# Batch 0 in pieces: keys as floats over SP, W_in in six loads, halves of tokens in the second softmax and first layer, and a new written order

## The chip, the cores and the metric

The kernel runs on one NeuronCore of a Trainium2 chip. Its engines are TensorE (PE; weight loads are shown as PEld), VectorE (DVE), ScalarE (ACT), GpSimd (POOL) and SyncE (SP). Each works through its own list of instructions, whose waits on semaphores hold up what stands behind them in the list. The core has 16 DMA engines, fed here from the queues of POOL, SP and, for the last store, ACT. The metric is the device time of one execution in microseconds, 251.08 us before the change (median of three runs, 250.28 to 251.39).

## The reference

Eight batches, eight heads, 576 tokens, head size 64, and 32 packed queries `p` per head. First `p` attends to `k` and `v`, then `q` attends to the packed result; the outcome, 4608 tokens by 512, goes through two layers with a squared ReLU between them.

```
def sm_attn(qq, kk, vv):
    s = scale * np.matmul(qq, kk.transpose(0, 1, 3, 2))
    s = s - np.max(s, axis=-1, keepdims=True)
    a = np.exp(s)
    a = a / (np.sum(a, axis=-1, keepdims=True) + 1e-09)
    return np.matmul(a, vv)
p_packed = sm_attn(p, k, v)
out = sm_attn(q, p_packed, p_packed)
...
h = x @ w_in            # x: 4608 x 512, w_in: 512 x 2048
r = np.maximum(h, 0.0)
g = r * r
return (g @ w_out).astype(np.float32)
```

## The kernel before

Work goes by batch and by quad, four heads of a batch (two quads). The second attention's product with the packed values is folded into the weights: `wp` is the packed values times W_in (32 x 4 rows for a quad, 2048 columns), and the first layer multiplies the second softmax `a2T` with `wp`. The second layer works on tiles of 128 tokens, `tt` 0 to 35, and 16 blocks `fb` of 128 hidden columns; `gT` holds the squared activations of four batches.

Nothing is scheduled by a planner at build time: the string `ORDER` is a list of words, read from left to right, and each word issues one step's instructions on its engines. So each engine's order is the order of the words that touch it. Digits after a word are batch and quad; a suffix `:a`, `:v`, `:p` names the engine (ACT, DVE, POOL).

- Loads: `Lk Lq Lv` (line 228, `load1`) through POOL with a cast from float to bf16, `Wi` and `Wo` (lines 219, 225) pieces of W_in (four, of 512 columns) and W_out, `Pr`, `Pt` the rest of p. `P0`, `P1` cast and transpose p of batches 0 and 1, which SP loaded as floats (line 170).
- First attention: `kT`, `qT` transpose a quad's keys and queries on DVE (lines 279, 285); `s1` scores (295), `m1` maximum (316), `x1` exponential (321), `rd` reciprocal (328), `eT` six transpositions on PE (339), `eo` their copy, `pv` (352), `pp` (360, 362), `bd` (367), `pt`, `po` (372, 376).
- Second attention: `s2` scores (295), `t2` transposition (383), `m2` (387), `sb` subtraction (391), `x2` (396), `su` sum and reciprocal (401, 403), `a2` multiplication (407), `aT` transposition (415).
- Layers: `w0`, `w1` form `wp` (422), `W0`, `W1` copy it out (332, 334), `h` first layer (438), `r` ReLU (444 on ACT, 446 on DVE), `q` square (479), `o` two of the 16 matmuls of a tile (490), `c` copy and store (500 to 510). For batch 0, `h0.fb` computes all 576 tokens in a pair of PSUM banks; for the others `hb.half.fb` computes 288.
- `Zn` issues n matmuls on zeros (263) that keep PE active; nothing reads them.

From batch 1 on, the attention of one batch stands among the layers of the batch before it. PSUM has eight banks: four for the attention (`psa`, two buffers of two banks), four that change use with the stage (`STAGES`). `PAIRED` names the batches whose two quads are computed on different parts of the PE array at once; their second quad's q is loaded in two halves. In the built program each POOL load from the ninth on waits until the eighth load before it has landed.

Of the kernel before, what the change touches and what calls it, by code (L numbers as in the profile page):

```python
# [627 lines left out]
```

## Time and profile before

| What | Value |
|---|---|
| Runs | 250.28, 251.08, 251.39 us |
| Span of the profiled execution | 248.6 us (first to last instruction; the page gives no other time for this execution) |
| PE busy | 237.1 us, 95% |
| of it matmuls on zeros | 14.4 us, 95 of them, all before 23.14 us |
| DVE, ACT, POOL busy | 194.2, 145.7, 45.8 us |
| First `s1`, first `h0`, first `h1` | 7.05, 23.15, 51.04 us |
| DMA through POOL | 18.55 MB; through SP 9.44 MB |

The span runs from the first to the last instruction; the runs' times also hold what lies around it. Busy time of an engine is the union of its instructions' times. The ends of matmuls are modelled by the profiler, and in its rows two in a row overlap. In groups of instructions the second number is the mean duration of one in ns; two instructions in a row on an engine may start closer together than that.

### The profile page before, as it was taken

What the parts mean: (1) busy time and instruction counts of PE and PEld (TensorE: products, weight loads), DVE (VectorE), ACT (ScalarE), POOL (GpSimd) and SP (SyncE); (2) the same over time, 40 slices, a digit from 0 to 9 for tenths busy, and PEclk for the clock granted to TensorE, in tenths of its full rate; (3) what the DMA queues carried; (4) which work ended last, traced back from release to release, by engine and by line L of the source; (5) the groups of instructions that cost most, each with busy time, mean ns of one, the idle gap of its engine ahead of it and who ended that gap; (6) DMA issues with size and microseconds to landing.
All of it is one profiled execution on the core that took longest, in us unless ns stands there. A gap on an engine that the chain in (4) does not pass through costs nothing.

```text
span 248.6 us, 6041 instructions
## 1 busy us (share of the span) xinstructions
PE 237.1 (95%) x2415; PEld 132.2 (53%) x2447; DVE 194.2 (78%) x411; ACT 145.7 (59%) x316; POOL 45.8 (18%) x75
## 2 busy tenths in 40 slices
PE   8998899998999999999999999999999999999992
PEld 5655554465556554655456555655555555555540
DVE  1888899978988899979887998898897798644710
ACT  2346784476968748755764658676957555353100
POOL 8329634350401500033000230010000000000000
PEclk9999999999999999999999999999999999999997
DMA  6999999999791992269812794252121213211323
GB/s 112 203 207 205 206 197 209 197 142 259 161 171 64 157 211 45 46 93 187 185 42 45 135 130 122 64 90 56 42 45 42 45 42 82 49 42 44 70 63 82
DMA packets 23358, 28.52 MB, mean 115 GB/s; under 512 B 4257, under 2 KB 14753, under 8 KB 23329
## 3 DMA queue, kind: packets, MB, share of 16 engines
q0 software_dynamic: 16880, 18.55, 47.1%
q1 hardware_dynamic: 6288, 9.44, 15.0%
q8 instruction: 19, 0.31, 0.5%
q10 hardware_dynamic: 160, 0.13, 0.2%
q14 instruction: 11, 0.08, 0.1%
HBM read 37.22 MB, written 9.44 MB: 188 GB/s over the span
## 4 chain that ended last, share of the span: by engine, by line
PE 81%; DMA 10%; issue 2%; DVE 2%; POOL 2%; ACT 1%; SPq 0%; ACTq 0%; POOLq 0%
PE ps_o L490 48%; PE ps_h L438 24%; DMA v_b<-in_v_dram 4%; PE ps_wp L422 3%; PE ps_s L295 3%; DMA w_in_bf<-in_moe_w_in_dram 3%; DMA out_dram<-o_sb 3%; PE ps_e1T L339 1%; PE ps_pv L352 1%; POOL k_b L242 1%; DVE mx L387 1%; POOL d L391 0%; ACT r L444 0%; POOL q_b L242 0%; PE ps_ppT L372 0%
## 5 line engine op out<-in xcount | busy, mean ns | idle before, releaser
L490 PE MATMUL ps_o<-w_out_bf,gT 128*128 128x512 bf16 x544 | 144.2, 379 | 2.0 <-issue 0.5
L444 ACT ACTIVATE r<-ps_h 128x288 bf16<-128x288 f32 (+1 forms) x181 | 73.1, 426 | 55.9 <-PE ps_h L438 47.5
L438 PE MATMUL ps_h<-a2T,wp 128*128 128x288 bf16 x512 | 91.9, 286 | 1.4 <-ACT r L444 1.4
L490 PEld LDWEIGHTS <-gT 128*128 128x128 bf16 x576 | 54.9, 98 | 42.1 <-issue 3.3
L438 PEld LDWEIGHTS <-wp 128*128 128x128 bf16 x512 | 47.4, 98 | 44.4 <-issue 7.7
L479 DVE TENSOR_TENSOR gT<-r 128x576 bf16<-128x576 bf16 x128 | 54.7, 448 | 5.2 <-ACT r L444 4.9
L446 DVE TENSOR_SCALAR r<-ps_h 128x288 bf16<-128x288 f32 (+1 forms) x59 | 28.5, 484 | 20.0 <-PE ps_h L438 18.8
L332 ACT CAST wp<-ps_wp 128x1024 bf16<-128x1024 f32 x29 | 28.9, 1016 | 3.8 <-PE ps_wp L422 3.7
L332 ACT COPY o_sb<-ps_o 128x512 f32<-128x512 f32 x27 | 15.9, 588 | 10.8 <-PE ps_o L490 9.4
L321 ACT ACTIVATE e<-ps_s,nm 128x576 bf16<-128x576 f32 x16 | 11.8, 736 | 13.0 <-DVE nm L316 13.0
L233 POOL DMA_DIRECT2D v_b<-in_v_dram x16 | 11.1, 695 | 44.2 <-PE ps_pv L352 22.5
L279 DVE STREAM_TRANSPOSE kT<-k_b 128x576 uint32<-128x576 uint32 x16 | 15.0, 943 | 5.1 <-DMA k_b<-in_k_dram 5.1
L263 PE MATMUL ps_idle<-nought 128*128 128x288 bf16 x95 | 14.4, 304 | 1.1 <-DVE nought L178 1.1
L383 DVE STREAM_TRANSPOSE s<-ps_s 128x576 f32<-128x576 f32 x16 | 12.0, 767 | 2.4 <-PE ps_s L295 2.4
L401 DVE TENSOR_REDUCE sums<-e 128x18 f32<-128x576 f32 x16 | 11.9, 741 | 1.4 <-ACT e L396 1.3
L242 POOL DMA_DIRECT2D k_b<-in_k_dram x16 | 9.0, 562 | 21.4 <-DVE kT L279 12.5
L422 PE MATMUL ps_wp<-w_in_bf,ppT 64*32 64x512 bf16 x256 | 11.4, 382 | 0.8 <-DMA w_in_bf<-in_moe_w_in_dram 0.7
L316 DVE TENSOR_REDUCE nm<-ps_s 128x1 f32<-128x576 f32 x16 | 11.6, 739 | 0.6 <-PE ps_s L295 0.6
L285 DVE STREAM_TRANSPOSE qT<-q_b 128x576 uint32<-128x576 uint32 x16 | 12.0, 761 | 0.0
L387 DVE TENSOR_REDUCE mx<-s 128x18 f32<-128x576 f32 x16 | 11.9, 743 | 0.1
L396 ACT ACTIVATE e<-d 128x576 f32<-128x576 f32 x16 | 11.0, 685 | 1.6 <-DVE d L391 1.4
L263 PEld LDWEIGHTS <-nought 128*128 128x128 bf16 x95 | 9.2, 103 | 4.9 <-issue 1.2
(47 smaller groups left out, 153.0 us busy)
## 6 DMA issues: line engine op xcount, KB each, us to landing
out_dram<-o_sb SPq DMA_DIRECT2D x70, 128.0 KB, 2.8
k_b<-in_k_dram POOLq DMA_DIRECT2D x16, 288.0 KB, 8.1
v_b<-in_v_dram POOLq DMA_DIRECT2D x16, 288.0 KB, 7.4
q_b<-in_q_dram POOLq DMA_DIRECT2D x10, 288.0 KB, 7.2
w_in_bf<-in_moe_w_in_dram POOLq DMA_DIRECT2D x4, 512.0 KB, 12.5
w_out_bf<-in_moe_w_out_dram POOLq DMA_DIRECT2D x4, 512.0 KB, 13.8
q_b<-in_q_dram POOLq DMA_DIRECT2D x12, 144.0 KB, 3.9
p_b<-in_p_dram POOLq DMA_DIRECT2D x1, 192.0 KB, 11.5
```

Source lines behind the costliest of these rows:

```text
L263: self.nc.tensor.matmul(ps[:, :HALF], lhsT=self.nought[:, :P], rhs=self.nought, start=True, stop=True)
L279: return self.nc.vector.transpose(t["kT"][:].rearrange("p (j l a) e -> p a j l e", j=J, a=3).bitcast(U32).rearrange("p a j l e -> p a j (l ...
L285: return self.nc.vector.transpose(t["qT"][:].rearrange("p s e -> p (s e)").bitcast(U32), t["q"][:].rearrange("p t d -> p (t d)").bitcast(U32))
L332: engine.copy(out, x)
L383: nc.vector.transpose(s2[:].rearrange("p (a t) i -> p a (t i)", a=2), t["ps_s2"][:, :, :HALF])
L387: self.nc.vector.tensor_reduce(out=t["mx"], in_=t["s2"], op=ALU.max, axis=AX.X)
L422: self.nc.tensor.matmul(ps[NP * h:NP * h + NP, c, :], lhsT=t["ppT"][D * c:D * c + D, NP * g:NP * g + NP], rhs=self.w_in_bf[D * c:D * c + D ...
L438: self.nc.tensor.matmul(ps, lhsT=t["wp"][:, fb // n, fb % n * P:(fb % n + 1) * P], rhs=t["a2T"][:, hf * HALF:(hf + 1) * HALF], start=(qd = ...
L444: engine.activation(r, ps, ACT.Relu)
L446: engine.tensor_scalar_max(r, ps, 0.0)
L479: (engine or self.nc.vector).tensor_tensor(out=out, in0=r, in1=r, op=ALU.mult)
L490: self.nc.tensor.matmul(self.o[tt], lhsT=self.gT[:, fb, a:a + P], rhs=self.w_out_bf[:, fb, :], start=(i == 0), stop=(i == self.NFB - 1))
```

## The change

- `Lk00` and `Lk01` load as floats through SP into the end of `gT`, not yet in use; `ka`, `kb` cast a half each to bf16, on ACT or DVE. SP's load of p becomes a word, `pf`, after `Lk00`.
- W_in comes in six pieces instead of four: columns 0 to 256, 256 to 512 and 512 to 1024 of each half. For batch 0 `w0` is split as well: `wa`, `wb` and their copies `Wa`, `Wb`.
- Batch 0's second softmax runs in tokens 0 to 320 (`tA mA sA xA uA aA TA`) and 320 to 576 (`tB` and so on), and batch 0's first layer is `h0.half.fb` on the same two parts, with one PSUM bank for each, ReLU per bank and a square per pair of blocks.
- The four stage banks have two uses instead of four: first `spare` and `idle`, then `x` and `y`, two banks each.
- Batch 1 joins the paired batches: `s11`, `s21` stand for both quads.
- `ORDER` is new throughout. There are 54 matmuls on zeros instead of 95, none of them before the first `s1`; in batches 1 to 7 POOL does 24 of the `sb` and `a2` steps instead of 3.

```diff
-PAIRED = range(2, 8)
+PAIRED = range(1, 8)
+
+PARTS = {False: ((0, HALF), (HALF, S)), True: ((0, 320), (320, S))}
...
-Lk00 Lk01 Lq00 kT00 P0 Z32 s100 kT01 I m100 x100 Z5 s101 m101 x101 Lq01 P1 Z7 eT00 Lv00 eo00:a Lk10 Z10 pv00 rd00
-qT00 rd01 qT01 pp00:v bd00 eT01 kT10 Lv01 Z3 s200 Wi00 Wi01 pt00 eo01:a Lk11 Z5 pv01 s110 pp01:a t200 pt01 Wi10 bd01
-m200 sb00:p m110 s201 x110 t201 x200 m201 su00 Z10 eT10 po01:v eo10:a a200:v Z12 w001 sb01:p po00:a x201 su01 Wi11
-aT00 w000 Lv11 a201:p kT11 W001:a Z11 s111 Lv10 W000:a aT01 h0.8 m111 h0.11 r0.8:a h0.9 r0.11:v h0.2 x111 r0.9:a
-w101 q0.8 h0.3 r0.2:v W101:a Lq11 eT11 eo11:a rd11 h0.10 Lq10 q0.9 rd10 w100 r0.3:v W100:a h0.1 r0.10:v h0.0 q0.3
-pv11 Wo0 r0.1:a q0.11 Pr r0.0:v h0.5 q0.2 pp11:a h0.6 pv10 r0.5:a qT11 r0.6:a pt11 bd11 q0.1 h0.14 pp10:a q0.10
-r0.14:a h0.12 s211 h0.15 q0.0 r0.12:a h0.7 r0.15:a po11:v qT10 r0.7:a w011 Wo2 t211 Lk21 h0.13 q0.6 W011:a q0.5 h0.4
-bd10 r0.4:a w111 s210 r0.13:v Wo1 o0.0 q0.7 m211 sb11:v o2.0 x211 W111:a t210 o2.1 Lk20 m210 o3.0 Wo3 o1.0 o0.1 o0.2
-q0.15 o1.1 su11 o1.2 Pt pt10 po10:a q0.4 o2.2 o3.1 w010 Lv20 w110 o0.3 Lq21 o3.2 o3.3 o0.4 q0.13 o2.3 W010:a Lv21
...
+Lk00 I pf Lk01 Lv01 Lq00 Lv00 Lq01 kb00:v ka00:a P0 Wi10 P1 Wi00 kT00 kb01:a ka01:a Wi11 s100 kT01 Wi01 m100 Wi21 Z3
+s101 x100 m101 Wi20 qT00 x101 Z7 eT00 rd00 eo00:v Z2 eT01 Lk11 rd01 eo01:v Z1 pv00 pp00:v Z1 pv01 bd00 pt00 Wo0 qT01
+s200 pp01:a po00:a bd01 pt01 tA00 po01:a s201 tB00 Lk10 mA00 tB01 sA00:p tA01 mB00 Lv11 mA01 mB01 xA00 sA01:p sB00:v
+Z17 wb00 wb01 sB01:v xB00 Lv10 uA00 xA01 Wb00:a Wb01:v Wo2 xB01 Z10 wa01 uA01 wa00 aA00:p Wa01:a uB01 Wa00:a aA01:p
+uB00 TA00 aB00:p TA01 aB01:v Z13 h0.0.2 Lq10 h0.0.8 h0.0.9 r0.0.2:v h0.0.3 r0.0.8:a TB00 h0.0.10 r0.0.9:a TB01
+r0.0.3:v h0.0.0 r0.0.10:a h0.0.1 r0.0.0:v q0.0.4:p h0.1.11 h0.1.2 r0.0.1:a q0.0.1:v h0.1.10 r0.1.11:a q0.0.0:v w100
+r0.1.2:a w101 r0.1.10:v W100:a Lq11 h0.0.11 W101:v h0.1.1 h0.1.8 h0.1.0 r0.0.11:a q0.1.5:p r0.1.1:a r0.1.8:v h0.1.3
+r0.1.0:a h0.1.9 q0.0.5:v r0.1.3:a h0.0.6 Wo1 kT11 r0.1.9:a h0.1.4 r0.0.6:a h0.0.7 h0.0.5 r0.1.4:a q0.1.0:p q0.1.1:v
+h0.0.4 r0.0.7:a r0.0.5:v h0.0.14 r0.0.4:a h0.1.5 q0.1.4:v h0.0.13 r0.0.14:a Pr q0.0.3:v h0.1.12 r0.1.5:a r0.0.13:v
+h0.0.12 r0.1.12:a h0.1.13 q0.1.2:p q0.0.2:v r0.0.12:a h0.1.15 kT10 h0.1.14 r0.1.13:a h0.1.6 r0.1.15:a h0.1.7 Wo3
+r0.1.14:a h0.0.15 q0.0.6:v r0.1.6:a s11 q0.1.6:v q0.1.7:p r0.1.7:v r0.0.15:a o3.0 m110 o1.0 q0.1.3:p q0.0.7:v o0.0
+x110 m111 o1.1 Lq21 o0.1 rd10 x111 eT10 o2.0 Lk20 eo10:v o3.1 rd11 pv10 eT11 Lv21 pp10:v o0.2 eo11:v pt10 o1.2 bd10
+po10:a pv11 qT10 Lk21 o1.3 pp11:a w010 w110 bd11 W010:v o0.3 W110:a Lq30 o3.2 o2.1 qT11 pt11 o3.3 po11:a s21 o2.2 t211
+o1.4 Lk31 t210 o2.3 o3.4 m211 Lq20 o0.4 m210 o2.4 sb11:p o0.5 Pt o3.5 sb10:v o1.5 x211 w011 x210 Lv20 o3.6 su11 W011:a
+o1.6 o3.7 su10 a211:p o0.6 c3:a o1.7 qT21 o0.7 Lv30 a210:v o2.5 c1:a Lq31 c0:a w111 aT11 aT10 o2.6 W111:a kT20 h1.0.0
+h1.0.1 o2.7 r1.0.0:a r1.0.1:v Lk30 h1.0.3 q1.0.0 h1.0.6 r1.0.3:a o4.0 kT21 r1.0.6:a h1.0.2 c2:a h1.0.4 r1.0.2:v Lk41
...
-        nc.sync.dma_start(self.p_f, self.packed(0, 2 * self.NQ))
...
-    STAGES = ((("spare", 3), ("idle", 1)), (("pair", 2),), (("pso", 2), ("early", 2)), (("psh", 2),))
+    STAGES = ((("spare", 3), ("idle", 1)), (("x", 2), ("y", 2)))
...
+    def bank(self, pool, name):
+
+        return self.banks(pool).tile([P, 512], F32, name=name, tag="t")
...
-    def load_w_in(self, c2, c):
-        f = c * (self.DFF // 2) + c2 * 512
+    def load_w_in(self, n, c):
+        f0, f1 = ((0, 256), (256, 512), (512, 1024))[n]
+        f = c * (self.DFF // 2)
         self.nc.gpsimd.dma_start(
-            self.w_in_bf[c * D:(c + 1) * D, :, c2 * 512:(c2 + 1) * 512],
-            self.w_in[:, f:f + 512].rearrange("(h d) f -> d h f", d=D))
+            self.w_in_bf[c * D:(c + 1) * D, :, f0:f1],
+            self.w_in[:, f + f0:f + f1].rearrange("(h d) f -> d h f", d=D))
...
+            if (n, b) == ("k", 0):
+
+                f = self.gT[:, self.NFB - 2:, :].rearrange("p f s -> p (f s)").bitcast(F32)[:, qd * T * D:(qd + 1) * T * D]
+                f = f.rearrange("p (t d) -> p t d", d=D)
+                self.nc.sync.dma_start(f, s)
+                self.att.setdefault((b, qd), {})["f"] = f
...
+    def st_cast(self, t, n, engine):
+        x = slice(n * T // 2, (n + 1) * T // 2)
+        self.copy(engine, t["k"][:, x, :], t["f"][:, x, :])
...
-    def scores(self, *quads):
-
-        for hf in range(2):
+    def scores(self, parts, *quads):
+
+        for hf, (s0, s1) in enumerate(parts):
-                        self.nc.tensor.matmul(ps[c, hf, :HALF], lhsT=x[r].rearrange("p (i e) -> p i e", e=2)[:, :, e],
-                                              rhs=y[r, hf * HALF:(hf + 1) * HALF, e], start=(e == 0), stop=(e == 1))
+                        self.nc.tensor.matmul(ps[c, hf, :s1 - s0], lhsT=x[r].rearrange("p (i e) -> p i e", e=2)[:, :, e],
+                                              rhs=y[r, s0:s1, e], start=(e == 0), stop=(e == 1))
...
-        self.scores(*x)
+        self.scores(PARTS[b == 0], *x)
...
+    def new(self, t, pool, name, shape, dt):
+        if name not in t:
+            t[name] = pool.tile(shape, dt, name=name)
+        return t[name]
...
+    def st_turn2(self, t, hf=None):
 
         nc = self.nc
-        s2 = t["s2"] = self.tp.tile([P, T, NP], F32, name="s2")
+        s2 = self.new(t, self.tp, "s2", [P, T, NP], F32)
+        if hf is None:
+            nc.vector.transpose(s2[:].rearrange("p (a t) i -> p a (t i)", a=2), t["ps_s2"][:, :, :HALF])
+        else:
+            s0, s1 = PARTS[True][hf]
+            nc.vector.transpose(s2[:].rearrange("p t i -> p (t i)")[:, s0:s1], t["ps_s2"][:, hf, :s1 - s0])
...
+    def span(self, hf):
+
+        s0, s1 = (0, S) if hf is None else PARTS[True][hf]
+        return slice(s0 // NP, s1 // NP)
...
+    def st_sub2(self, t, engine, hf=None):
+        x = self.span(hf)
+        d2 = self.new(t, self.tp, "d2", [P, T, NP], F32)
+        n = x.stop - x.start
+        engine.tensor_tensor(out=d2[:, x], in0=t["s2"][:, x], in1=t["mx"][:, x].unsqueeze(2).to_broadcast([P, n, NP]),
...
+    WP = {"0": (0, 512), "a": (0, 256), "b": (256, 512), "1": (512, 1024)}
+
+    def st_wp(self, t, b, qd, n):
+        f0, f1 = self.WP[n]
+        ps = t["ps_wp", n] = self.turn32("ps_wp")
...
-                self.nc.tensor.matmul(ps[NP * h:NP * h + NP, c, :],
+                self.nc.tensor.matmul(ps[NP * h:NP * h + NP, c, :f1 - f0],
-                                      rhs=self.w_in_bf[D * c:D * c + D, QH * qd + h, c2 * 512:(c2 + 1) * 512],
+                                      rhs=self.w_in_bf[D * c:D * c + D, QH * qd + h, f0:f1],
...
-    def step_h(self, engine, b, *x):
-
-        if b == 0:
-            fb, = x
-            ps = self.ph[b, fb] = self.banks("pair").tile([P, 2, 512], F32, name="ps_h2")
-            for hf in range(2):
-                self.layer1(ps[:, hf, :HALF], b, fb, hf)
...
+    def step_h(self, engine, b, hf, fb):
+
+        s0, s1 = PARTS[b == 0][hf]
+        ps = self.ph[b, hf, fb] = self.bank("y" if b or fb % 2 else "x", "ps_h")
+        self.layer1(ps[:, :s1 - s0], b, fb, s0, s1)
...
+    def step_r(self, engine, b, hf, fb):
+        s0, s1 = PARTS[b == 0][hf]
+        if (b, hf, fb // 2) not in self.r:
+            self.r[b, hf, fb // 2] = self.rp.tile([P, 2, 320], BF16, name="r")
+        self.relu(engine, self.r[b, hf, fb // 2][:, fb % 2, :s1 - s0], self.ph.pop((b, hf, fb))[:, :s1 - s0])
+
+    def step_q(self, engine, b, hf, fp):
+
+        s0, s1 = PARTS[b == 0][hf]
+        r = self.r.pop((b, hf, fp))[:, :, :s1 - s0]
         c = (b % 4) * S
-        if b == 0:
-            out, r = self.gT[:, x[0], c:c + S], r[:].rearrange("p a s -> p (a s)")
-        else:
-            c += x[0] * HALF
-            out = self.gT[:, 2 * x[1]:2 * x[1] + 2, c:c + HALF]
+        out = self.gT[:, 2 * fp:2 * fp + 2, c + s0:c + s1]
...
-            self.o[tt] = self.banks("early" if tt < 2 else "pso").tile([P, self.NE], F32, name="ps_o")
+            self.o[tt] = self.bank("y" if tt < 2 else "x", "ps_o")
...
+        elif word == "pf":
+            self.nc.sync.dma_start(self.p_f, self.packed(0, 2 * self.NQ))
```

## The prediction

> **What bounds the kernel now.** First the page: TensorE is busy 237.1 of 248.6 us, so the time is TensorE's work plus the stretches in which it has none.
>
> ```profile
> PE 237.1 (95%) x2415; PEld 132.2 (53%) x2447; DVE 194.2 (78%) x411; ACT 145.7 (59%) x316; POOL 45.8 (18%) x75
> ```
>
> Then the table of windows, cut where the stages change (columns: length; busy PE, PEld, DVE, ACT, POOL; clock, DMA share, GB/s). The first h0 starts at 23.15 us, the first h1 at 51.04.
>
> ```profile
> 0.00:23.14 23.14, 20.55 (x275) 13.06 (x275) 15.30 (x31) 9.76 (x16) 12.86 (x23) 1.00 1.07 180
> 23.14:30.00 6.86, 5.86 (x58) 3.54 (x54) 5.21 (x11) 4.67 (x8) 5.01 (x8) 1.00 1.24 206
> 30.00:37.28 7.28, 7.04 (x131) 4.25 (x129) 6.88 (x17) 6.16 (x12) 2.92 (x5) 1.00 1.43 198
> 37.28:51.04 13.76, 13.60 (x106) 5.79 (x106) 13.50 (x23) 6.50 (x11) 6.27 (x9) 1.00 1.15 193
> 51.04:60.00 8.96, 8.05 (x139) 5.14 (x139) 6.99 (x19) 6.20 (x15) 1.96 (x4) 1.00 1.09 208
> 90.00:232.80 142.80, 141.49 (x1358) 78.81 (x1377) 116.97 (x254) 88.27 (x200) 9.31 (x16) 1.00 0.40 79
> ```
>
> From 90 us on TensorE has no more than 1.31 us idle in 142.8: nothing is to be won there. Of the 20.55 us busy before 23.14, filler is 14.44 (the same windows for `ps_idle`). So the change is decided by when h0 starts, and how well TensorE is fed from there to h1. Next the chain of waits (start, length, what), start-up part:
>
> ```profile
> 5.27 9.11 DMA v_b<-in_v_dram
> 14.42 0.40 PE ps_pv L352 x24
> ...
> 17.48 0.76 DVE mx L387
> ...
> 18.31 1.10 POOL d L391
> 19.41 7.36 DMA w_in_bf<-in_moe_w_in_dram
> 26.82 0.41 PE ps_wp L422 x7
> ```
>
> Two loads, then VectorE and GpSimd. TensorE itself lost only 0.3 us to v and 0.7 us to W_in (the list of waits). Prices are from groups by form and the timeline. Back to back an instruction costs less than its duration, here start to start: the maximum over 128x576 0.67 (16.01 to 16.68; a transposition of that size is taken as 0.68), the gT square 0.40 (two in 0.81), the 288-column ACT relu 0.30 (two in 0.71). From ACT's relus of 288 and 576 columns, 412 and 653 ns, a column costs 0.84 ns; the 1024-column cast is 0.92 (two in 1.93). An instruction that needs the one just before pays its whole duration and 0.03.
>
> ```profile
> 16.01 0.75 DVE L316 TENSOR_REDUCE nm<-ps_s 128x1 f32<-128x576 f32 x1
> 16.68 0.77 DVE L383 STREAM_TRANSPOSE s<-ps_s 128x576 f32<-128x576 f32 x1
> 17.48 0.75 DVE L387 TENSOR_REDUCE mx<-s 128x18 f32<-128x576 f32 x1
> 29.36 0.81 DVE L479 TENSOR_TENSOR gT<-r 128x576 bf16<-128x576 bf16 x2
> 54.16 0.71 ACT L444 ACTIVATE r<-ps_h 128x288 bf16<-128x288 f32 x2 [0.20 <-PE ps_h L438]
> L444 ACT ACTIVATE r<-ps_h 128x576 bf16<-128x576 f32 x10 | 6.2, 653 | 2.4 <-issue 1.4 <-PE ps_h L438 1.0
> L415 DVE STREAM_TRANSPOSE a2T<-a 128x288 uint32<-128x288 uint32 x16 | 7.0, 457 | 0.2
> p_f<-in_p_dram SPq DMA_DIRECT2D x1, 128.0 KB, 2.2
> ```
>
> The sum is made against the profiled execution's span, 248.6; the median of the runs is 251.08, so 2.5 us lie around it.
>
> **Stage 1, start to h0.** Call E the end of the second key transposition kT01 (now 8.12; h0 follows 15.03 later).
>
> Removed: two k loads at the head of POOL's queue (0.56 each to issue), so v and q are issued at once, from about 1.8 us, and the six W_in pieces (0.71 each, two more than now) by about 8.5 us. The p casts stay (0.25 each, transposition 0.25). Added on SP: k00, p, k01 (0.45 each to issue). Two keys of 590 KB and p's 131 KB go over the same DMAs. p_f's row gives 2.2 us to landing and the windows show its data from about 2.0 us. Rate, from both sides: the POOL loads run at 198 GB/s written as bf16, 396 read; the output stores at 9.44 MB / (15.0% x 248.6 us) = 253. Fast, alone: k00 at 4.1, k01 at 2.0 + 1311 KB / 396 + 0.35 = 5.7. Slow and shared: 9.5. I take the fast rate (a load of long rows, as the POOL loads) and half of it from 4.2 us, when v's data come: (1311 - 870) KB / 198 = 2.2, so k01 at 6.7. Then ACT's two casts (by the 512-column copy's 0.59 and ACT's slope, 0.54 + 0.64), kT01 0.95: E = 8.9. kT00 is done by 6.5 behind a VectorE cast (0.45; between 0.25, p's cast, and 0.69, the 512-column copy) and both p casts, so k01 is what counts; m100 is queued behind kT01 on VectorE and waits with it.
>
> From E on VectorE sets the pace: m100 and the wait for s101 0.80, m101 0.67, qT00 0.68, two reciprocals and two eT copies to 3.55, pp 0.38, bd 0.13, qT01 0.69, bd01 0.13: tA00 starts at E + 4.9. Halves: from 288 and 576 columns a transposition has 0.10 fixed, so 320 columns cost 0.42 and 256 0.36. Eight half transpositions and maxima 3.1, two half subtractions 0.7, the first sum and reciprocal 0.7, Wb01 0.6, three sums 1.85, two a2T pieces 0.55, release 0.1: h0 at E + 12.6. GpSimd's halves (0.7 each, of 1.19) and ACT's run beside it. If the pieces paid whole durations (halves 0.48 and 0.42) it is E + 14.0.
>
> Fillers: 95 become 54, and none stands before s100. In the timeline the first five took 1.38 us, twelve later ones 1.77: 0.26 against 0.14 each, though the clock column says 1.00. So s100, s101 and part of Z7 run slow: between 0 and 1.4 us on the chain, 0.5 taken. h0 = 8.9 + 12.6 + 0.5 = 22.0 (now 23.15).
>
> The Trainium skill, TensorE: Matmul & The Clock Gate, Part 1, says the array starts throttled until about 3.4 us of activity have passed; by that all of s100 to Z7 would be slow, the 1.4. The fillers' rows agree in kind (slow for some 2.6 us).
>
> POOL: in the built order each load from the ninth on waits for the landing of the eighth before it, and sA00, sA01, aA00, TA's source, stand behind such loads. At 0.2 MB per us W_in's first four pieces land by 16.7; Wo2, which waits for the last and has aA00 behind it, comes at E + 9.3 = 18.2. Cost 0, 1.5 us of cover; without it, rival 3.
>
> **Stage 2, h0 to h1.** I walked the new order step by step, in time from h0. TensorE has 16 x 0.27 + 16 x 0.22 of h0, 0.67 for w100 w101, 0.65 for s11: 9.2. ACT has 24 relus of 0.33 or 0.27 and a 0.92 cast: 8.1; VectorE 8 relus (0.40, 0.35), 9 squares (0.45, 0.36), W101 1.13, kT11 and kT10 0.85 each, two TB: 10.3. VectorE wins: s11 waits for kT10 and starts at 9.7, ends at 10.4. The four banks keep ACT, and so TensorE, just ahead of that. The 14 o steps with eT, pv and w (8.2, and 0.3 of waits) lead to s21, which ends at 19.5. Then VectorE's chain: t2, t2, m2, m2 2.7, Pt 0.56 + 0.97, sb 0.68, su, su 1.9, qT21 0.69, a2 0.70, aT 0.39 + 0.46: 9.1. TensorE has 17 o and two w for 8.0 of it and waits 1.1: h1 at 28.75.
>
> Now that stage takes 27.89, at 28 o steps and batch 2's first scores done; then 31 o steps without them, 3 x 0.432 - 0.63 = 0.67 more work done. The pairing of batch 1 (32 matmuls in 0.63, now 16 in 0.62, twice) is in this.
>
> **Stage 3.** 24 multiplications and subtractions of batches 1 to 7 run on GpSimd (3 now): 1.17 each for 0.78, off VectorE. Priced 0: a batch's attention runs one batch ahead of its use and TensorE has o steps meanwhile; where that cover is gone, 0.4 each. A walk of h1's first 9 us loses 0.4 (now 0.91). Unknown, taken as 0, with 1 us either way. Tail: the order now ends with o33 and o35 mixed, so c33's copy and stores come 1.7 us ahead of c35's (3.45 us now, o34 to o35); 0 to 0.3, taken as 0.
>
> **Sum.** 22.0 + 28.75 - 0.67 - 51.04 = -0.96; span 247.6, time 250.1.
>
> **Rivals.** 1, faster: the keys come unshared, k01 at 5.7. E = 7.9, h0 at 21.0, time 249.1; the pieces' fixed part also hidden or h1's 0.5 won, 248.5. For it: p_f landed in 2.2 us; v's data cannot come before about 4. 2, slower: k01 at 9.5, E = 11.7, clock 0.9: h0 at 25.2, +2.2: 253.3. It decides (over 0.5%) from h0 at 24.2, k01 at 8.7. Against: the POOL loads' rate is higher than the stores'.
>
> The Trainium skill, DMA: Bandwidth & Descriptors, Issuing engines are not separate DMA queues, says a DMA from another engine shares the same 16 and only saves issue time; it speaks for rival 2, and the DMA share of 1.0 to 1.2 before 23 us agrees.
>
> 3, slower: W_in's 512-byte rows take a packet's mean time (47.1% x 248.6 x 16 / 16880 = 0.11 us) as the 1 KB rows do. 1024 more packets / 16 engines: 7.1 us, Wi01 at 23.8, aA00 behind it, h0 near 26.5: 254.6. Against: p's 1536 small packets landed 0.6 us after the W_out piece ahead of them. 4, no change: h0 comes when it came, as W_in's landing was no wait of weight (0.7 us): -0.96 + 1.1, 251.2.
>
> **Chances.** Forecast 0.45 (249.0 to 251.2; 0.5%, about what a measurement here can tell, is 1.25 us and cuts it near 249.8: 0.2 faster, 0.25 same); rival 1 0.2, faster; 2 0.2 and 3 0.07, slower; 4 0.08, same, of which 0.03 drifts to slower. Faster 0.40, same 0.30, slower 0.30. The range reaches from rival 1's lower end to rival 2's upper, 248.2 to 253.6; the forecast's own is 249.0 to 251.2.
>
> **What would show it.** kT01's end near 8.9; first h0 near 22 with TA01 before it; s11's end some 10.4 us later, released by kT10; a wait of about 1 us at the first h1 released by aT10; SP's k loads landing by 5 and 7 us; POOL waiting for no DMA ahead of sA00 to aA01. I am wrong if k01 lands after 8.7, if GpSimd is late for TA, or if stage 3 loses more than 1 us over today's.

## The result

The changed kernel takes 259.23 us (median of four runs, 257.41 to 261.17) where the kernel before takes 251.24 beside it: 1.0305 times as long, 95% interval 1.0229 to 1.038. Its profiled execution took 258.58 with a span of 256.8, against 248.6 before. The forecast was 250.1, in a range of 248.2 to 253.6: wrong in sign and outside the range. An execution that ran over 1.5% longer than the fastest of its kernel (one of e2's and one of e4's below) is left out of times and ratios.

The page of the changed kernel first: TensorE was busy 237.1 us before and is now 235.9 in a span 8.2 longer, and VectorE is busy 16.5 us more (194.2 before) although GpSimd took over some of its work (45.8 before). The new order also moves work from ScalarE (145.7 before) to VectorE: 91 relus there against 59, and 11 copies of wp against 3. No run below gives any of this back to ScalarE.

```profile
PE 235.9 (92%) x2422; PEld 128.9 (50%) x2422; DVE 210.7 (82%) x449; ACT 128.6 (50%) x287; POOL 79.0 (31%) x105
```

The windows, cut at the first h0 (24.95), batch 1's first scores (37.08), the first h1 (55.95) and then as in the prediction (length; busy PE, PEld, DVE, ACT, POOL; clock, DMA share, GB/s):

```profile
0.00:24.95 24.95, 15.52 (x213) 9.90 (x214) 14.95 (x40) 8.76 (x18) 14.60 (x27) 1.00 1.13 204
24.95:37.08 12.13, 9.54 (x81) 6.16 (x79) 12.12 (x22) 8.60 (x24) 9.12 (x12) 1.00 1.21 207
37.08:55.95 18.87, 18.49 (x221) 7.90 (x221) 16.62 (x32) 8.35 (x17) 11.34 (x16) 1.00 1.20 192
55.95:66.00 10.05, 7.44 (x83) 4.63 (x83) 7.58 (x15) 6.09 (x16) 1.46 (x4) 1.00 1.00 211
```

In the second window VectorE is busy for 12.12 of 12.13 us and TensorE only for 9.54; in the last TensorE stands for 2.6 of 10 us (0.9 of 9 before). The list of TensorE's waits names who is late:

```profile
PE ps_s L313 <- DVE kT L297: 8.9, 2, 6.5
PE ps_h L482 <- DVE r L489: 3.0, 3, 1.8
PE ps_h L482 <- ACT r L487: 2.6, 2, 2.4
```

And the chain of waits through these stages (start, length, what): a key's load in place of v's and W_in's, then VectorE nearly all the way, among it squares (L509), and a store of 6.40 us.

```profile
1.66 6.95 DMA gT<-in_k_dram
...
9.91 0.95 DVE kT L297
10.90 1.15 PE ps_s L313 x16
12.04 1.79 PE ps_idle L277 x7
...
30.48 1.93 DVE gT L509
...
54.81 6.40 DMA out_dram<-o_sb
```

As the two orders mix their steps differently, equal stretches do not hold equal work. The table below takes the work out. Every weight load of TensorE is given the spacing, start to start, that its kind has in unbroken stretches of the traces (0.216 us for an o, 0.121 for an h, 0.067 for a transposition of e1, 0.037 for a W_in product, 0.020 for a score, 0.011 for a v product); a stretch's loss is its length less that sum (the prices are rounded here; with the rounded ones the last column comes out some 0.35 lower in every run alike). "Start" is up to the first h0, fillers counted as loss.

| us lost | start | h0 to h1 | h1 to h2 | h2 to last h |
|---|---|---|---|---|
| before | 18.8 | 3.8 | 1.6 | 2.1 |
| changed | 20.9 | 5.6 | 3.4 | 4.1 |
| changed, run again (e5) | 21.2 | 6.3 | 5.1 | 4.1 |

So 2.1 + 1.8 + 1.75 + 2.0 us were lost in four different places, and 0.6 is the price of 16 more of W_in's products (272, 256 before, the first ones in pieces of 256 columns); the end costs 5.0 in both. Together that is the 8.2. The 0.6 is hardly more work: sixteen products of 256 columns take 0.34 us to the next matmul (20.57 to 20.91), sixteen of 512 take 0.56 (44.48 to 45.04), so that some 0.5 of it belongs to the start. The second profile of the same kernel shows what varies from run to run: the middle columns most, the last not at all.

### The profile page after: what moved, and what is told of

It reads as the page before. It is cut to its first block, busy times and chain, and to the rows that moved or that the text cites. A ratio compares the mean times of both kernels' runs of the same rounds, so it can differ in the third digit from the quotient of the medians.

```text
span 256.8 us, 6106 instructions
## 1 busy us (share of the span) xinstructions
PE 235.9 (92%) x2422; PEld 128.9 (50%) x2422; DVE 210.7 (82%) x449; ACT 128.6 (50%) x287; POOL 79.0 (31%) x105
## 4 chain that ended last, share of the span: by engine, by line
PE 69%; DVE 18%; DMA 5%; ACT 3%; issue 2%; SPq 1%; POOL 0%; ACTq 0%; POOLq 0%; DVEq 0%
PE ps_o L520 40%; PE ps_h L482 19%; DVE gT L509 5%; PE ps_s L313 3%; DMA gT<-in_k_dram 3%; DMA out_dram<-o_sb 2%; PE ps_e1T L357 2%; DVE mx L420 2%; PE ps_wp L466 2%; PE ps_pv L370 2%; DVE s L407 2%; DVE r L489 2%; DVE wp L352 1%; DVE sums L438 1%; PE ps_idle L277 1%
## 5 line engine op out<-in xcount | busy, mean ns | idle before, releaser
L482 PE MATMUL ps_h<-a2T,wp 128*128 128x288 bf16 (+2 forms) x512 | 91.7, 286 | 5.7 <-DVE r L489 3.0
L487 ACT ACTIVATE r<-ps_h 128x288 bf16<-128x288 f32 (+2 forms) x165 | 63.4, 411 | 63.5 <-PE ps_h L482 57.0
L482 PEld LDWEIGHTS <-wp 128*128 128x128 bf16 x512 | 47.7, 98 | 49.9 <-issue 11.9
L509 DVE TENSOR_TENSOR gT<-r 128x576 bf16<-128x576 bf16 (+2 forms) x122 | 60.6, 520 | 5.6 <-ACT r L487 4.5
L489 DVE TENSOR_SCALAR r<-ps_h 128x288 bf16<-128x288 f32 (+2 forms) x91 | 40.1, 450 | 14.0 <-PE ps_h L482 13.3
L426 POOL TENSOR_TENSOR d<-s,mx 128x576 f32<-128x576 f32 (+1 forms) x15 | 17.1, 1147 | 64.6 <-DVE mx L420 64.5
L350 ACT CAST wp<-ps_wp 128x1024 bf16<-128x1024 f32 (+1 forms) x23 | 21.5, 958 | 2.7 <-PE ps_wp L466 2.6
L350 ACT COPY o_sb<-ps_o 128x512 f32<-128x512 f32 x23 | 13.4, 586 | 15.1 <-PE ps_o L520 11.8
L446 POOL TENSOR_TENSOR a<-e,rs 128x576 bf16<-128x576 f32 (+2 forms) x14 | 15.2, 1088 | 10.9 <-DVE rs L440 10.0
L432 ACT ACTIVATE e<-d 128x576 f32<-128x576 f32 (+2 forms) x18 | 11.0, 630 | 8.5 <-POOL d L426 7.0
L352 DVE CAST wp<-ps_wp 128x1024 bf16<-128x1024 f32 (+1 forms) x11 | 12.7, 1159 | 0.4 <-PE ps_wp L466 0.3
L438 DVE TENSOR_REDUCE sums<-e 128x18 f32<-128x576 f32 (+2 forms) x18 | 11.9, 661 | 0.0
## 6 DMA issues: line engine op xcount, KB each, us to landing
w_in_bf<-in_moe_w_in_dram POOLq DMA_DIRECT2D x4, 256.0 KB, 11.7
```

What stands on the lines that cost most here:

```text
L350: engine.copy(out, x)
L352: engine.tensor_copy(out, x)
L426: engine.tensor_tensor(out=d2[:, x], in0=t["s2"][:, x], in1=t["mx"][:, x].unsqueeze(2).to_broadcast([P, n, NP]), op=ALU.subtract)
L438: nc.vector.reduce_sum(out=sums[:, x], in_=t["e2"][:, x], axis=AX.X)
L446: engine.tensor_tensor(out=a2[:, y].rearrange("p t i e -> p t e i"), in0=t["e2"][:, x].rearrange("p (t e) i -> p t e i", e=2), in1=t["rs"] ...
L482: self.nc.tensor.matmul(ps, lhsT=t["wp"][:, fb // n, fb % n * P:(fb % n + 1) * P], rhs=t["a2T"][:, s0:s1], start=(qd == 0), stop=(qd == se ...
```

## The experiments

All theories start from that table: which cause sits in which column. The results of all runs stand together here; the columns are the losses just defined, and the ratio is to the kernel before on the same chip.

| run | time, us | ratio, 95% | start | h0 to h1 | h1 to h2 | h2 to last h |
|---|---|---|---|---|---|---|
| e5 changed again | 260.47 | 1.0338 (1.0291-1.0384) | 21.2 | 6.3 | 5.1 | 4.1 |
| e1 squares on VectorE | 257.0 | 1.0216 (1.017-1.0263) | 21.1 | 3.6 | 4.5 | 4.1 |
| e2 fillers first | 256.72 | 1.0219 (1.0179-1.0258) | 20.0 | 5.6 | 3.1 | 4.1 |
| e3 six out buffers | 256.3 | 1.0204 (1.0177-1.0231) | 20.5 | 6.2 | 0.8 | 4.1 |
| e4 keys by GpSimd | 256.96 | 1.0217 (1.0151-1.0282) | 18.2 | 5.2 | 2.5 | 4.1 |
| e6 the four together | 252.6 | 1.0042 (1.0025-1.0059) | 19.0 | 3.7 | 0.8 | 4.1 |
| e7 and 22 steps to VectorE | 261.58 | 1.0412 (1.0383-1.0442) | 19.7 | 4.6 | 0.7 | 13.1 |
| e8 loads held back | 259.26, one run | | 21.5 | 5.7 | 3.3 | 4.1 |
| e9 three subtractions | 253.39 | 1.006 (1.0037-1.0084) | 18.7 | 4.3 | 0.7 | 4.9 |
| e10 one key each way | 251.82 | 1.0013 (0.9987-1.0039) | 17.6 | 4.4 | 0.7 | 4.9 |
| e11 softmax whole | 261.21, one run | | 21.2 | 6.7 | 4.6 | 4.1 |
| e12 two subtractions | 250.95 | 0.9968 (0.9941-0.9995) | 17.9 | 4.3 | 0.7 | 3.5 |

**The changed kernel again (e5)**, without an edit.

> The changed kernel itself once more, to have it beside the others on one chip. Every theory: the first h0 near 25, the first h1 31 us later, a wait of about 2.4 us near 62 us, time 257.5 to 259.3.

It took 260.47, above what was expected: h0 at 25.24, h1 31.7 later, the wait 2.52 us at 63.3. The pattern is the same. What differs is the granted clock, third from the end in a window's line. The stretch from 64 to 70 us, in the changed kernel's first profile and in e5:

```profile
64.00:70.00 6.00, 6.00 (x106) 3.75 (x104) 5.77 (x16) 4.42 (x11) 1.89 (x3) 1.00 0.69 134
```

```profile
64.00:70.00 6.00, 6.00 (x83) 3.60 (x81) 4.19 (x10) 4.07 (x11) 0.53 (x1) 0.74 0.56 123
```

At 0.74 for 6 us TensorE loses 0.26 x 6 = 1.6 us, the 5.1 instead of 3.4 in the table. A narrower window of e5 shows that the clock was halved for 3.41 us:

```profile
63.69:67.10 3.41, 3.41 (x12) 1.52 (x10) 1.71 (x5) 2.27 (x6) 0.00 (x0) 0.50 0.86 207
```

The same 3.41 us at 0.50 stand at 36.38 in e5 (its 6.3 before h1), at 59.84 in e1, 35.26 in e3, 15.77 in e7, 17.34 in e8, 36.84 and 64.14 in e11, and nowhere in the changed kernel's first profile before its end. They go with the spread of its times: of its eight executions the three with a mean clock of 0.997 or more took 257.41 to 258.67, the five at 0.983 to 0.985 took 259.81 to 261.36. So differences of under 2 us in the columns are read only where this clock agrees.

**Squares (e1).** What to see first, in the changed kernel's timeline of VectorE and GpSimd (start, length):

```profile
27.27 1.41 DVE L509 TENSOR_TENSOR gT<-r 128x640 bf16<-128x640 bf16 x2
...
30.40 2.00 DVE L509 TENSOR_TENSOR gT<-r 128x640 bf16<-128x640 bf16 x1
...
33.85 1.49 DVE L509 TENSOR_TENSOR gT<-r 128x512 bf16<-128x512 bf16 x2
...
35.66 0.47 DVE L509 TENSOR_TENSOR gT<-r 128x640 bf16<-128x640 bf16 x1
```

```profile
26.68 1.25 POOL L509 TENSOR_TENSOR gT<-r 128x640 bf16<-128x640 bf16 x1 [0.75 <-ACT r L487]
...
29.17 1.03 POOL L509 TENSOR_TENSOR gT<-r 128x512 bf16<-128x512 bf16 x1 [0.17 <-DVE r L489]
30.16 0.82 POOL L234 DMA_DIRECT2D w_out_bf<-in_moe_w_out_dram  x1
30.99 1.05 POOL L509 TENSOR_TENSOR gT<-r 128x512 bf16<-128x512 bf16 x1
...
33.62 1.03 POOL L509 TENSOR_TENSOR gT<-r 128x512 bf16<-128x512 bf16 x1 [0.55 <-ACT r L487]
```

A square alone takes 0.47 (35.66). The first of the two at 27.27 takes 1.01 of their 1.41 and ends 0.35 after GpSimd's square did (27.93); the square at 30.40 ends 0.36 after GpSimd's (32.04); the pair at 33.85 likewise holds one of 1.08. So VectorE does its square only when GpSimd has finished.

```
- q0.0.4:p ... q0.1.5:p ... q0.1.0:p ... q0.1.2:p ... q0.1.7:p ... q0.1.3:p
+ q0.0.4:v ... q0.1.5:v ... q0.1.0:v ... q0.1.2:v ... q0.1.7:v ... q0.1.3:v
```

> The six squares of batch 0 that the changed kernel gives to GpSimd go back to VectorE; nothing else changes. Theory 'lock' (a VectorE multiplication of two SBUF operands cannot run beside a GpSimd one and waits for its end; in the changed kernel the ten VectorE squares of batch 0 take 8.5 us together, the longest 2.00): with GpSimd's squares gone all sixteen take 0.40 to 0.45 (640 columns) and 0.36 to 0.38 (512), 6.5 us together, so VectorE has LESS to do although it gets six more squares; from the first h0 to batch 1's first scores 10.1 us instead of 12.1, time about 257.2. Rival 'work' (VectorE is overloaded in that stretch and the long squares are its own): six squares of 0.4 are added, the stretch takes 14.5 us, time about 261.6.

The squares by form, of the changed kernel and of e1:

```profile
L509 DVE TENSOR_TENSOR gT<-r 128x640 bf16<-128x640 bf16 x7 | 5.8, 834 | 0.0
...
L509 DVE TENSOR_TENSOR gT<-r 128x512 bf16<-128x512 bf16 x3 | 2.7, 904 | 0.0
```

```profile
L509 DVE TENSOR_TENSOR gT<-r 128x640 bf16<-128x640 bf16 x8 | 3.7, 477 | 0.0
L509 DVE TENSOR_TENSOR gT<-r 128x512 bf16<-128x512 bf16 x8 | 3.1, 405 | 0.0
```

Sixteen squares now take 6.8 us where ten took 8.5. From h0 to batch 1's first scores it is 10.8 us (12.1, and 12.9 in e5), from h0 to h1 29.0 (31.0). "Lock" holds, "work" falls: taking six squares (some 2.5 us) off the engine that sets the pace had slowed it. A grouping over the whole trace of the changed kernel says which instructions are held (VectorE's mean ns, by what GpSimd did for over 30% of the time):

| changed kernel, VectorE | GpSimd idle | issuing a DMA | in a tensor_tensor |
|---|---|---|---|
| square, both operands in SBUF, 576 columns | 448 (78) | 444 (13) | 693, up to 1414 (19) |
| relu from PSUM, 288 | 453 (64) | 440 (8) | 435 (9) |
| sum over 576, from SBUF | 742 (4) | 721 (3) | 727 (7) |

The Trainium skill has this: SBUF — State Buffer, Who interferes with whom, says that a VectorE instruction with two SBUF inputs and a GpSimd instruction that reads SBUF take a shared port pair as an exclusive lock, and that whichever comes second waits for the other's whole instruction. The trace agrees (1414 against 448). It also says that issue order decides, and the 19 that overlap bear it out: they range from 393 up. The kernel before had one such square too, hidden in a mean of 448; its timeline, VectorE and GpSimd:

```profile
41.79 1.05 DVE L217 TENSOR_SCALAR pT<-pT 128x768 bf16<-128x768 bf16 x1
42.76 1.77 DVE L479 TENSOR_TENSOR gT<-r 128x576 bf16<-128x576 bf16 x2
```

```profile
41.47 1.15 POOL L407 TENSOR_TENSOR a<-e,rs 128x576 bf16<-128x576 f32 x1 [1.02 <-DVE rs L403]
42.59 1.26 POOL L391 TENSOR_TENSOR d<-s,mx 128x576 f32<-128x576 f32 x1
```

The first of the two squares at 42.76 took 1.40 of the 1.77, and pT's scaling at 41.79, 1.05, was held as well: it ends 0.22 after GpSimd's multiplication did (42.62). In the changed kernel it takes 0.36, but it is not alone there either; it begins 0.13 before GpSimd's subtraction ends (51.09) and ends 0.24 after that:

```profile
49.94 1.15 POOL L426 TENSOR_TENSOR d<-s,mx 128x576 f32<-128x576 f32 x1 [2.23 <-DVE mx L420]
50.96 0.36 DVE L224 TENSOR_SCALAR pT<-pT 128x768 bf16<-128x768 bf16 x1
```

In all fourteen profiles it ends 0.22 to 0.24 after a GpSimd operation, however early it began; what it takes alone no run shows.

**Fillers (e2).**

```
- ... Wi11 s100 ...      - ... Z3 s101 ...
+ ... Wi11 Z26 s100 ...  + ... Z24 s101 ...
```

> 26 filler matmuls stand ahead of s100 and 24 in place of 3 ahead of s101, where TensorE waits for the keys anyway. Theory 'cold array' (TensorE has had no work, so its first matmuls run at half the pace although the clock column says 1.00): s100 and s101 take 0.69 instead of 1.15, the first seven fillers behind them 1.0 instead of 1.86, the two eT of batch 0 0.53 instead of 0.85 each; the first h0 comes 1.4 us earlier, at 23.5, time about 257.8. Rival 'VectorE sets the pace': the matmuls get as fast but the first h0 stays within 0.4 us of 24.95, time 258.9 to 259.3.

TensorE at batch 0's second scores and behind, in the changed kernel and in e2:

```profile
10.90 1.15 PE L313 MATMUL ps_s<-kT,pT 32*32 32x288 bf16 x16 [2.39 <-DVE kT L297]
11.98 1.86 PE L277 MATMUL ps_idle<-nought 128*128 128x288 bf16 x7
13.63 0.85 PE L357 MATMUL ps_e1T<-ident,e 128*96 128x128 bf16 x6
```

```profile
11.44 0.69 PE L313 MATMUL ps_s<-kT,pT 32*32 32x288 bf16 x16 [0.91 <-DVE kT L297]
12.06 1.03 PE L277 MATMUL ps_idle<-nought 128*128 128x288 bf16 x7
12.92 0.52 PE L357 MATMUL ps_e1T<-ident,e 128*96 128x128 bf16 x6
```

From the second key transposition's end to h0 it is 12.64 us in e2, and 13.4 to 14.1 in the four runs with the old fillers (the changed kernel twice, e1, e3). In e10, warm as well, it is 13.37, of which 0.74 is waiting for q. So the cold array costs 0.7 to 1.5 us, all of it on the chain; h0 itself comes at 24.02, as the key landed at 9.15 there and at 8.61 in the changed kernel's profile. Both columns of windows call the clock 1.00.

**Stores (e3).** ScalarE in the changed kernel and in e3:

```profile
61.31 0.59 ACT L350 COPY o_sb<-ps_o 128x512 f32<-128x512 f32 x1 [3.21 <-DMA out_dram<-o_sb]
```

```profile
58.23 0.59 ACT L350 COPY o_sb<-ps_o 128x512 f32<-128x512 f32 x1
```

The fourth copy of output rows waits 3.21 us for the store that still holds one of the three buffers, and the relus behind it in ScalarE's list, then TensorE, wait with it. The kernel before has the same wait in small, at stores that land no faster (one copy on ScalarE; the six stores issued from 50 to 55 us, median us to landing):

```profile
58.59 0.59 ACT L332 COPY o_sb<-ps_o 128x512 f32<-128x512 f32 x1 [1.44 <-DMA out_dram<-o_sb]
```

```profile
out_dram<-o_sb SPq DMA_DIRECT2D x6, 128.0 KB, 7.3
```

What the new order adds is that the copies stand closer: the fourth is due 4.6 us after the first began (53.51 to 58.10), before it was 7.2 (49.9 to 57.15).

```
- self.op = pool("op", 3)
+ self.op = pool("op", 6)
```

> The output rows get six buffers instead of three. Theory 'store': TensorE's wait of 2.45 us at 62.3 us stands behind ACT's third copy of output rows, which waits 3.2 us for the store that still holds its buffer (6.4 us from issue to landing there): the wait goes, and the time falls by 2.0 to 2.5, to about 257.0. Rival: another thing is late by then (VectorE's squares or batch 2's scores), most of the wait comes back within the next 20 us, time 258.5 to 259.2.

The wait is gone and nothing takes its place: every run with six buffers loses 0.7 to 0.8 us from h1 to h2, those with three 2.5 to 5.1. (e6's rival below reads e1's 4.5 in this column as a gain given back. It is not: the wait there is 2.06, and the clock 0.79 from 56 to 64 us.)

**Keys (e4, e8).**

```
- Lk00 I pf Lk01 Lv01 Lq00 Lv00 Lq01 kb00:v ka00:a P0 ... kT00 kb01:a ka01:a
+ Lk00 Lk01 I pf Lv01 Lq00 Lv00 Lq01 P0 ... kT00
- if (n, b) == ("k", 0):     (the float load on SP)
+ if (n, b) == ("k", -1):
```

> Batch 0's keys come as bf16 by GpSimd's queue as in the kernel before, ahead of all else, without casts; p alone by SP; all else as in the changed kernel. Theory 'late key' (the second float key lands at 8.6 us beside v's loads, and the chain starts from its transposition, whose end is at 10.85): the transposition ends at 8.1 to 8.7 as before, the first h0 14.1 us later, at 22.2 to 22.8, time about 256.9. Rival 'the queue': v, q and W_in come 1.1 us later and one of them is what the chain then waits for, the first h0 at 24 to 25, time within 0.5 us of 259.2.

The second key transposition ends at 8.35 (10.85 to 11.7 with float keys) and h0 comes at 22.24, 13.9 us after that: "late key" holds. (The profiled execution is e4's fastest, 254.78, 2.2 us ahead of the next; the 18.2 in the table is its alone.) In e8 it is shown what made the key late:

```
- Lk00 I pf Lk01 Lv01 ... kT00 kb01:a ka01:a
+ Lk00 I pf Lk01 kb01:p Lv01 ... kT00 ka01:a
```

> The changed kernel, but the upper half of key quad 1 is cast by GpSimd ahead of v's and q's loads, so that these are only issued once both keys have landed. Theory 'shared' (the float keys have the DMA engines at some 400 GB/s until v's data come, and half of it after): alone, the second key lands at 5.5 to 6.0 us instead of 8.6 to 9.5. Rival 'slow by itself' (float loads on SP run at the stores' rate of 250 GB/s): it lands at 7.5 to 8.5. In both the later loads come some 6 us late, and the first h0 with them, so the time says nothing.

It lands at 6.87, between the two expectations; 8.61 to 9.48 beside v's and q's loads. Windows of e8 (last column GB/s; nothing but the keys and p is moving):

```profile
2.00:3.00 1.00, 0.00 (x0) 0.00 (x0) 0.00 (x0) 0.03 (x1) 0.00 (x0) 1.00 0.93 364
3.00:4.20 1.20, 0.00 (x0) 0.00 (x0) 0.00 (x0) 0.00 (x0) 0.00 (x0) 1.00 1.04 316
4.20:5.20 1.00, 0.00 (x0) 0.02 (x1) 0.94 (x4) 0.67 (x1) 0.00 (x0) 1.00 0.80 272
```

Alone the keys get 364 falling to 272 GB/s, where 396 was forecast throughout, and sharing costs another 1.7 to 2.6 us. In the changed kernel they are alone until 5.2 us as well (401, 277 and 305 GB/s in the same windows). From 5.2 to 6.9 us their queue (q1) moves 0.18 MB, 105 GB/s, beside GpSimd's (q0):

```profile
q0 software_dynamic: 233, 0.18, 76.1%
q1 hardware_dynamic: 52, 0.18, 31.7%
```

The transposition then ends at 8.61 in e8, but h0 comes at 25.53 all the same, as q, issued 6 us later, holds up VectorE for 2.64 us and v TensorE for 3.17: the loads cannot simply be put behind each other either.

**The four together (e6)**: the edits of e1, e3 and e4, with Z30 ahead of s100 and Z5 ahead of s101.

> The changed kernel with the squares of batch 0 on VectorE, batch 0's keys by GpSimd's queue, six output buffers, and fillers ahead of s100 (30) and s101 (5). Theory 'four separate losses' (each alone took 2.0 between h0 and h1, 2.7 ahead of h0, 2.6 between h1 and h2, and 0.8 to 1.6 ahead of h0): they add up, 8.1 to 8.9 us off the changed kernel's 256.8 span, so time 250.0 to 251.2, within 0.5% of the kernel before. Rival 'one behind the other' (what is won in one stretch is lost in the next, as the squares' gain was cut from 2.0 to 0.6 by the wait at 60 us): at most half comes through, time near 254.5.

252.6 with a span of 250.5: 6.3 us off the changed kernel's 256.8, where "four separate losses" promised 8.1 to 8.9 and its rival at most half, so neither holds as written. The h0-to-h1 and h1-to-h2 gains add up in full (3.7, 0.8). The start does not: h0 comes 14.6 us after the second transposition, because with both keys in GpSimd's queue q is late, and VectorE waits for it:

```profile
11.71 0.78 DVE L303 STREAM_TRANSPOSE qT<-q_b 128x576 uint32<-128x576 uint32 x1 [1.36 <-DMA q_b<-in_q_dram]
...
14.53 0.78 DVE L303 STREAM_TRANSPOSE qT<-q_b 128x576 uint32<-128x576 uint32 x1 [0.35 <-DMA q_b<-in_q_dram]
```

The same loads brought q 0.8 us earlier in e4's profile (10.88, 11.69 here), so part of this varies between executions.

**The later batches (e7, e9, e12).** From h2 on the loss was 4.1 in every run so far, 2.1 before. The first trial is e6 with these words changed:

```
- sb20:p ... a270:p   (22 words of batches 2 to 7)
+ sb20:v ... a270:v
```

> As e6, and the 18 subtractions and multiplications of batches 2 to 7 that the changed kernel gives to GpSimd are VectorE's. Theory 'lock goes on' (from the first h2 on TensorE loses 2.0 us more than in the kernel before, the same in all five runs so far, because VectorE's squares wait for GpSimd's operations): it comes down by 1 to 2 us, time 249 to 250. Rival 'VectorE has no room' (18 x 0.78 = 14 us more for an engine that is busy 126 of 145 us there, with an order that has counted on GpSimd): it loses 1 us or more, time over 251.5.

(There are 22 such steps, not 18: 17 us for VectorE.) "No room" holds, with 13.1 us lost. So a GpSimd step that holds squares can still be cheaper than the same step on VectorE. The middle way, again from e6, is to move only those behind which a square stands.

```
- sb20:p ... sb51:p ... sb71:p
+ sb20:v ... sb51:v ... sb71:v
```

> As the four mends together (252.6), and three of GpSimd's subtractions, one each in batches 2, 5 and 7, are VectorE's: those beside which a VectorE square takes 1.2 to 1.4 us instead of 0.44. Theory 'lock' (where a square stands behind GpSimd's subtraction, the subtraction costs VectorE 0.8 to 1.0 us anyway, more than the 0.75 of doing it): TensorE's loss from the first h2 to the last h comes down from 4.1 to about 3 us, time 251.3 to 251.9. Rival 'no room' (22 moved operations cost 9 us, so each one costs 0.4): three cost 1.2, time 253.8.

4.9 instead of 4.1: neither theory. Batch 7's won 0.29 (from h6 to h7 0.66 instead of 0.95), batch 2's nothing, and batch 5's lost 1.1 from h5 to h6. The last was picked wrongly: the held square at 121 us stands beside batch 4's subtraction.

**One key each way (e10)**, on top of e9: the second key alone by GpSimd, ahead of v and q; the first stays on SP as floats.

```
- Lk00 Lk01 I pf Lv01 ... P0
+ Lk00 pf Lk01 I Lv01 ... kb00:v ka00:a P0
- if (n, b) == ("k", -1):
+ if (n, b, qd) == ("k", 0, 0):
```

> As the run with three subtractions on VectorE, but key quad 0 comes as floats over SP, as in the change, and only key quad 1 by GpSimd's queue, ahead of v and q. Theory 'queue' (with both keys in GpSimd's queue q is late, VectorE waits 1.4 and 0.35 us for it): q comes up to 1 us earlier, the first h0 at 22.0 to 22.5 instead of 23.0, time 250.4 to 251.2. Rival 'shared' (the same bytes and more come over the same engines in the same time, 590 KB of floats where 590 KB were read before): key quad 1 lands at 7.5 as before and q no earlier, the time stays within 0.4 of the other run.

The key lands at 7.30, VectorE waits for q 0.39 and 0.35 instead of 1.36 and 0.35, h0 comes at 21.64; "queue" holds. The time, above the 250.4 to 251.2 expected, is 1.6 below e9's, with the same wrong subtraction in it.

**The second softmax (e11)**: tA/tB, mA/mB and so on replaced by whole steps (t2, m2, sb, x2, su, a2, aT), the first layer still in pieces.

> The changed kernel with batch 0's second softmax in one piece per quad as in the kernel before (W_in and the first layer stay in pieces). Theory 'pieces start h0 earlier': the first h0 comes 14.5 to 15.1 us after the second key transposition's end instead of 13.4 to 14.1. Rival 'fixed costs' (VectorE has twice as many instructions with 0.1 us fixed each, and it is what sets the pace): 13.0 to 13.8, and 0.5 us less from the first h0 to batch 1's first scores, where two transpositions of second pieces fall away.

14.43 us from the transposition to h0, against 13.4 to 14.1: by this one execution the pieces bring 0.3 to 1.0 us, a little less than the first theory said, and cost nothing that shows behind it (13.0 us from h0 to batch 1's scores, 12.0 to 13.2 in the runs with pieces and GpSimd's squares). W_in's six pieces, the first layer in halves and the pairing of batch 1 were not tried by themselves.

**Two subtractions (e12)**: as e10, with sb41 and sb71 on VectorE, sb20 and sb51 back on GpSimd.

> As the run with one key each way (span 250.6), but of the three moved subtractions batch 2's and batch 5's are GpSimd's again (no square stood behind batch 5's: the trace has the 1.41 us square at 121 us beside batch 4's), and batch 4's first is VectorE's beside batch 7's. Theory 'lock': batch 5's subtraction cost 1.1 us (the stretch from h5 to h6 lost 2.3 instead of 1.2), and batch 2's made GpSimd's queue late at 46 us, so that the scaling of pT stood behind GpSimd's subtraction there (1.06 us instead of 0.46); both come back, and where the square stood behind batch 4's subtraction 0.2 is won: span 248.6 to 249.2, time 250.0 to 250.6, ratio to the kernel before 0.994 to 0.997. Rival 'no room': any subtraction on VectorE costs 0.4, wherever it stands, so the time stays at 251.4 or above.

VectorE at the place of batch 4's held square, in e6 (two squares, the second 1.41) and in e12:

```profile
120.53 1.77 DVE L509 TENSOR_TENSOR gT<-r 128x576 bf16<-128x576 bf16 x2
```

```profile
120.05 0.44 DVE L509 TENSOR_TENSOR gT<-r 128x576 bf16<-128x576 bf16 x1
120.41 0.75 DVE L426 TENSOR_TENSOR d<-s,mx 128x576 f32<-128x576 f32 x1
121.08 0.45 DVE L509 TENSOR_TENSOR gT<-r 128x576 bf16<-128x576 bf16 x1
```

Batch 5's 1.1 us are back, and batch 4 and batch 7 win 0.29 each, so the column is 3.5. The part on batch 2 fell: pT's scaling still takes 0.86, so batch 2's subtraction was not what made GpSimd late there. Batch 1's subtraction on GpSimd starts right behind the issue of a q load (45.12 to 45.65) and ends at 46.83, 0.63 after the scaling began; in the changed kernel that issue is over 2.2 us before the subtraction. Why the load is issued so late in e12 is open. At 250.95 against 251.74, ratio 0.9968 (0.9941 to 0.9995), this version is the fastest of all, 0.3% ahead of the kernel before, which is less than the half per cent that the prediction set as the limit of what can be told from no change. Its profiled span, 249.4, is 0.8 above that of the kernel before.

## Why the prediction was wrong

**What bounds the kernel** was read right as far as it went: the change was decided by h0 and by how TensorE is fed up to h1. Of the time from 90 us on, "nothing is to be won there" was true, but 2.0 us could be lost from h2 on.

**Stage 1, "k01 at 6.7".** This step failed: it was sized at the POOL loads' 396 GB/s, then half. The changed kernel's keys got 401, 277 and 305 alone, then 105; they landed at 6.87 alone (e8), at 8.6 to 9.5 shared. That is rival 2's case, whose decision point of 8.7 the profile missed by 0.09 and the five other runs with that key passed. E came at 10.85 for 8.9. This term alone is 1.95 us of the 2.95 by which h0 (24.95) missed 22.0.

**Stage 1, "E + 12.6" and "0.5 taken".** The walk was right (its terms add to 12.5): 12.64 once the array was warm (e2). The clock's term, 0.7 to 1.5, was undersized; the Trainium skill's rule (TensorE: Matmul & The Clock Gate, Part 1), by which the sum would have had 1.4, was the better price, and the row of fillers pointed the same way. POOL's cost of 0 was right: its wait ahead of sA00 ended with VectorE's maximum (2.94 us), none with a load; rival 3 did not come.

**Stage 2, "9 squares (0.45, 0.36)".** This step failed too: the squares were priced from a row in which GpSimd is almost always idle, and GpSimd's own squares were priced at nothing for VectorE. The order has eight squares on VectorE ahead of s11, not nine, and ten in all. The eight, 3.4 at those prices, took 6.3, and all ten 8.5; TensorE waited 2.4 (1.76 and 0.68) for VectorE's relus behind them, and s11 began 12.1 after h0 for 9.7. With all sixteen on VectorE the stage takes 29.0, 0.25 above the forecast's 28.75 (whose terms add to 28.6). The predicted 1.1 us of waiting at the first h1 for aT10 did not come in the changed kernel (0.50 in e12; TensorE's own steps from s21 to h1 took 8.3), partly because pT's scaling took 0.36, not 0.97.

**Stage 3, "loses 0.4" and "priced 0".** This is the largest miss: two terms priced at next to nothing lost 3.8 us more than in the kernel before. The walk of h1's first 9 us allowed for no wait for an output buffer; the store that held it took 6.4 us to land, as in the kernel before, but with the copies closer together three buffers made ScalarE wait: 2.45 us of TensorE. That the store is slow because GpSimd's loads of v, q and k start beside it (51 to 59 us) was not tried. From h2 on, under the new order and with 24 steps on GpSimd, 2.0 us more are lost than before: 0.6 of it goes when two GpSimd subtractions with a square behind them move to VectorE (0.29 each, e12), for the rest the trace shows only that TensorE's longest waits there end with a VectorE square (0.29 at 194.7), a VectorE relu (0.60 at 215.5) and a ScalarE copy (0.27 at 131.9). The steps could not simply be given back (e7), as the order leaves VectorE no room for them.

**The sum.** The span came out 9.2 us above the forecast's 247.6: 2.95 before h0, 2.25 from h0 to h1, 4.0 behind h1. Each of the three stages was allowed to be late alone; the range had no case in which all three are. The changes in h0 and in h1 do add: the lost microseconds of four columns stand one after another in the span.

## What to carry to other kernels

Giving GpSimd a share of elementwise work is no free relief for VectorE where both read two operands from SBUF: look in the trace of before for a single long instance of VectorE's operation beside GpSimd's, not at the row's mean, and move only what no two-operand VectorE instruction stands behind. Taking all of it back is no remedy either where the written order has no room for it (e7). A load moved to another queue still shares the DMA engines, so a transfer that the chain starts from should go first and carry as few bytes as it can. Where TensorE waits at the start anyway, put its filler ahead of the first matmuls that count.

## What the runs showed of the hardware

- VectorE's square of two SBUF operands waits for GpSimd's tensor_tensor to end: 0.44 becomes up to 1.41, and once 2.00 (30.40 us), where the square began in the 0.8 us between two of GpSimd's squares in which GpSimd issued a DMA, and still waited for the second. What held it in that gap isn't shown; DMA issues without a square behind them hold nothing (444 ns). It also works the other way: GpSimd's subtraction of 1.16 takes up to 1.37 where it begins during a VectorE square (163.03 us).
- The scaling of pT, one SBUF operand of bf16, is held in the same way: where it began 0.2 to 1.1 us before the end of a GpSimd operation (six profiles) it took 0.46 to 1.32 and ended 0.22 to 0.23 after that end. The Trainium skill's section named above (SBUF — State Buffer, Who interferes with whom) lists such a tensor_scalar among those that can contend. Relus from PSUM and sums are not held.
- The first matmuls run at about half pace (1.15 for sixteen scores, 0.69 when warm; a filler 0.26, then 0.14) while the record of the granted clock says 1.00 throughout.
- The granted clock fell to 0.50 for 3.41 us at a time, eight times in six of the fourteen profiles before TensorE's last matmuls (e1, e3, e5, e7, e8, e11). Each time it began during a wait of TensorE of 1.6 to 3.2 us, or within 2.5 us after one. The changed kernel's first profile has such waits too (1.76, 2.45) and stayed at 1.00; what decides it isn't shown.
- Two loads by different queues at once slowed each other: 590 KB of key landed at 6.9 us alone and at 8.6 to 9.5 beside v and q.
